# Key-value products in 32-column tiles, and one visit a period with outputs, key-value products and the next pair's scores

## The chip, the cores and the metric

The kernel runs on one core of a Trainium2 chip. The metric is the device time of one execution in microseconds, the median of three runs. Times from a profile are counted from the first instruction of the profiled execution.

## The reference

A linear attention with a decaying state (RWKV-5) is followed by a two-layer network with a leaky ReLU. Batch 4, 8 heads, 768 tokens, 48 channels a head; the network goes from 384 to 2048 and back to 384.

```python
state = np.zeros((B, H, D, D), dtype=np.float32)
for t in range(S):
    cur = np.einsum('bhd,bhe->bhde', u[None] * kt, vt)
    y[:, :, t] = np.einsum('bhd,bhde->bhe', rt, state + cur)
    state = w[None, :, :, None] * state + np.einsum('bhd,bhe->bhde', kt, vt)
...
h = x @ w_in
g = np.maximum(0.01 * h, h)
return (g @ w_out).astype(np.float32)
```

Here x holds y with the heads of a token side by side, and the output has 3072 rows of 384.

## The kernel before

The 768 tokens are cut into 6 chunks of 128, and a **stage** n (0 to 23) is one chunk of one batch element: chunk n // 4 of batch n % 4. So the state that stage n leaves is wanted by stage n + 4. A head's 48 channels are padded to 64 where two heads share the 128 rows of an operand, and four such pairs of heads make a stage.

The order of all work is written out by hand in the string ORDER (L27 to L52). Each word names a step and its stage; the steps are recorded in that order, each engine runs its own steps in that order, and `Sched` (L61) puts a semaphore wait before a step whose inputs, or whose buffer, belong to an earlier step of another engine. A wait holds up everything behind it on its engine. The steps that matter here:

- k, r, v (L241): loads, issued by GpSimd. P (L390): VectorE scales r and k by powers of the decay into `qk`. X (L395): SyncE issues a transposing DMA from `qk` to `tp`.
- A (L482): scores, 8 matmuls a stage on TensorE with 48 rows by 128 columns of weights, into two PSUM banks. M (L495): VectorE writes them masked into `at`, a half (a, b) at a time. Before that q (L419 to L423, VectorE) and Q (L430, GpSimd, two instructions of 128x512 a stage) have put the diagonal there.
- Y (L621): the outputs, 28 matmuls a stage with 128 rows by 32 columns of weights. They go round four groups of 32 columns of the array, so that four run side by side, each with 128 moving columns. y (L635): ScalarE copies them to `xT`.
- K (`kv_mm`, L516): the sums of key times value, 4 matmuls a stage (L523), one a pair of heads, with 128x128 weights and 96 moving columns. The off-diagonal blocks, of one head's key with the other's value, are computed too and are made zero later by the table `wl`. S (`state`, L580): VectorE adds the bank to the old state `st` (L589, 128x384) and multiplies by `wl` (L591) into the state of stage n + 4.
- J (L660): the first layer for a pair of stages, in eight parts of 6 matmuls with 256 moving columns; j (L671): ScalarE's leaky ReLU of each part into `gT`. H (L684): the second layer for one stage, 16 matmuls with 384 moving columns; h (L696): ScalarE's copy, and an output DMA issued by SyncE.

`take` (L213) hands out the PSUM bank that has been free longest, and `give` (L217) returns one when the step that reads it is recorded; so a J part can wait for the reader of the bank that it gets.

From stage 8 on two stages make a **period**: 2 A, 2 Y, 2 K, 2 H and 8 J on TensorE. In a period such as that of 10 and 11 the order on TensorE is H6, Y10 Y11, K10 K11, H7, J5.0 to J5.7, with the next scores A12 A13 after it; from the next period on, A14 A15 stand between J6.2 and J6.3. A run of steps Y, K or A between J and H is called a **visit** below. The order early in the kernel is not regular; around stages 6 and 7 it is Y7 y7 K5 r11 K6 S6 r10 k10 S5 Q9 v8 K7 S7 h0 h3 k11 J3.0.

Of the kernel before, what the change touches and what calls it, by code (L numbers as in the profile page):

```python
# [26 lines left out]
ORDER = """  # L27
w8 qk0 k0 v0z one r0 trow ones v0y tcol wlz r1 id8 F9 wi1 u8 zr table Cw Wl id E w bc lnw c0q@ T0q c0k@ tri u exps k1
T0k u16 wu8 Cu t0q t0k qtab P1q F6 k3 v3 U A0 ktab T1q v0 t1q X0 C D0 P1k T1k t1k F4 M0b P3k M0a T3k K3 utab X1 A1 D1
Q0 Y0 t3k P0k r3 P3q M1a T3q r2 P2q y0 k2 K0 M1b v1 Q1 W G0.1 Y1 t3q X3 wi3 A3 y1 g0.1 S3 T2q D3 G1.1 g1.1 k5 t2q r5 r4  # L30
P2k T2k wi2 S0 v2 M3b t2k Q3 G0.3 g0.3 G1.3 k4 M3a Y3 P5k A2 y3 P4q T4q v4 wi0 T5k v5 wo3 t4q g1.3 G3.1 q5 t5k Q5 G3.3
g3.3 P5q r6 wo2 X2 g3.1 M2b D2 wo1 G3.2 Q2 G0.2 g0.2 T5q t5q K2 P4k T4k M2a t4k S2 G1.2 g3.2 q4 Q4 K1 S1 Y2 A5 A4 G1.0
y2 G2.1 M5a G0.0 G2.3 M4a M5b Y5 g0.0 y5 M4b Y4 y4 G2.2 g2.2 K4 J2.4 j2.4 k6 wo0 J2.1 J2.2 g1.0 g1.2 S4 k7 P6q q6 j2.1
P6k P7k G2.0 r7 q7 X6T J2.6 j2.6 J2.3 j2.3 k8 G3.0 J2.7 j2.7 k9 r9 j2.2 J2.5 P7q g3.0 g2.3 X7T J2.0 H1 h1 r8 q8 g2.0 Q6
P9k j2.0 P8k H0 j2.5 H3 Q7 A6 P9q X9T P8q X8T v6 A7 M6a v7 M7a g2.1 H2 h2 v9 v11 v10 M6b Y6 M7b y6 Q8 q9 Y7 y7 K5 r11
K6 S6 r10 k10 S5 Q9 v8 K7 S7 h0 h3 k11 J3.0 j3.0 J3.1 j3.1 J3.2 j3.2 J3.3 j3.3 J3.4 j3.4 J3.5 j3.5 J3.6 j3.6 J3.7 j3.7
A8 A9 M8a M8b M9a M9b P10q P10k X10T P11q P11k X11T k12 r12 v12 k13 r13 v13 q10 Q10 q11 Q11 H4 h4 Y8 Y9 y8 y9 K8 K9 S8
S9 H5 h5 J4.0 j4.0 J4.1 j4.1 J4.2 j4.2 J4.3 j4.3 J4.4 j4.4 J4.5 j4.5 J4.6 j4.6 J4.7 j4.7 A10 A11 M10a M10b M11a M11b
P12q P12k X12T P13q P13k X13T k14 r14 v14 k15 r15 v15 q12 Q12 q13 Q13 H6 h6 Y10 Y11 y10 y11 K10 K11 S10 S11 H7 h7 J5.0
j5.0 J5.1 j5.1 J5.2 j5.2 J5.3 j5.3 J5.4 j5.4 J5.5 j5.5 J5.6 j5.6 J5.7 j5.7 A12 A13 M12a M12b M13a M13b P14q P14k X14T  # L40
P15q P15k X15T k16 r16 v16 k17 r17 v17 q14 Q14 q15 Q15 H8 h8 Y12 Y13 y12 y13 K12 K13 S12 S13 H9 h9 J6.0 j6.0 J6.1 j6.1
J6.2 j6.2 P16q P16k X16T P17q P17k X17T A14 A15 J6.3 j6.3 M14a M14b M15a M15b k18 r18 v18 k19 r19 v19 J6.4 j6.4 J6.5
j6.5 J6.6 j6.6 J6.7 j6.7 q16 Q16 q17 Q17 H10 h10 Y14 Y15 y14 y15 K14 K15 S14 S15 H11 h11 J7.0 j7.0 J7.1 j7.1 J7.2 j7.2
P18q P18k X18T P19q P19k X19T A16 A17 J7.3 j7.3 M16a M16b M17a M17b k20 r20 v20 k21 r21 v21 J7.4 j7.4 J7.5 j7.5 J7.6
j7.6 J7.7 j7.7 q18 Q18 q19 Q19 H12 h12 Y16 Y17 y16 y17 K16 K17 S16 S17 H13 h13 J8.0 j8.0 J8.1 j8.1 J8.2 j8.2 P20q P20k
X20T P21q P21k X21T A18 A19 J8.3 j8.3 M18a M18b M19a M19b k22 r22 v22 k23 r23 v23 J8.4 j8.4 J8.5 j8.5 J8.6 j8.6 J8.7
j8.7 q20 Q20 q21 Q21 H14 h14 Y18 Y19 y18 y19 K18 K19 S18 S19 H15 h15 J9.0 j9.0 J9.1 j9.1 J9.2 j9.2 P22q P22k X22T P23q
P23k X23T A20 A21 J9.3 j9.3 M20a M20b M21a M21b J9.4 j9.4 J9.5 j9.5 J9.6 j9.6 J9.7 j9.7 q22 Q22 q23 Q23 H16 h16 Y20 Y21
y20 y21 H17 h17 J10.0 j10.0 J10.1 j10.1 J10.2 j10.2 A22 A23 J10.3 j10.3 M22a M22b M23a M23b J10.4 j10.4 J10.5 j10.5
J10.6 j10.6 J10.7 j10.7 H18 h18 Y22 Y23 y22 y23 H19 h19 J11.0 j11.0 J11.1 j11.1 J11.2 j11.2 J11.3 j11.3 J11.4 j11.4  # L50
J11.5 j11.5 J11.6 j11.6 J11.7 j11.7 H20 h20 H21 h21 H22 h22
"""  # L52


# [89 lines left out]
def bass_rwkv5_eagle__then__act_leaky_relu_kernel(  # L144
# [370 lines left out]

    def kv_mm(n):  # L516
        iq = n % NQK
        ps_kv, key = kv_bank[n] = take()
        carried = NB <= n < CARRY

        def emit():
            for p in range(NP):
                last = PE.matmul(ps_kv[:, 96 * p:96 * p + 96],  # L523
                                 qk[iq][:, H + 2 * p:H + 2 * p + 2, :].rearrange("p h e -> p (h e)"),
                                 v_sb[:, n, :].rearrange("p (h e) -> p h e", e=E)[:, 2 * p:2 * p + 2, 0:D],
                                 start=p == 0 or not carried, stop=not carried)
# [52 lines left out]

    def state(n):  # L580
        ps_kv, key = kv_bank[n]
        give(key)
        kv = ps_kv[:, 0:HD].rearrange("p (m e) -> p m e", e=2 * D)
        new = st[(n + NB) % NT]
        if n < NB or n < CARRY:
            add("dve", lambda: V.tensor_tensor(new[:, :, :], kv, wl[:, :, :], ALU.mult),
                R=[key, "wl0", "wl1"], W=[("st", (n + NB) % NT)])
        else:
            add("dve", lambda: V.tensor_tensor(sum_t[n % 4][:, :, :], kv, st[n % NT][:, :, :], ALU.add),  # L589
                R=[key, ("st", n % NT)], W=[("sum", n % 4)])  # L590
            add("dve", lambda: V.tensor_tensor(new[:, :, :], sum_t[n % 4][:, :, :], wl[:, :, :], ALU.mult),  # L591
                R=[("sum", n % 4), "wl0", "wl1"], W=[("st", (n + NB) % NT)])
# [212 lines left out]
```

## Time and profile before

| | |
|---|---|
| median of three runs | 168.86 us (168.78 to 168.94) |
| span of the profiled execution | 166.8 us, first to last instruction |
| PE busy | 160.2 us, 96% of the span |
| VectorE (DVE), GpSimd (POOL), ScalarE (ACT) busy | 107.6, 111.0, 89.0 us |
| granted TensorE clock | 1.000 over the span |

The runs' times are taken without a profile; what the profiled execution took in all is not listed beside its span of 166.8 us; the median of the runs lies 2.0 us above that span. PE in the profile is TensorE's matmuls and PEld its weight loads. Matmuls are pipelined: a row's duration holds the time that a matmul takes through the array (some 0.2 us) beside its share of the stream, so distances between starts tell the rate. A row "x8" in a timeline reaches from the first start to the last end of eight.

### The profile page before, as it was taken

The numbers are of one execution on the slowest core, as the hardware profiler recorded it, in microseconds if no ns is written. First come the engines' busy times: TensorE is split into PE (matmuls) and PEld (weight loads), VectorE is DVE, ScalarE is ACT, GpSimd is POOL, SyncE is SP. The second block draws the span as 40 slices with busy tenths as digits, with TensorE's granted clock in tenths as the row PEclk, the third lists the DMA queues.
The fourth block names the chain that finished last, engine by engine and source line by source line (L and its number), as shares of the span: only waits on it lengthen the run. The fifth ranks groups of instructions, "written<-read, shape, count | busy, mean of one in ns | idle before, by whom it ended". The sixth has DMA issues, their size and how long they took to land.

```text
span 166.8 us, 4840 instructions
## 1 busy us (share of the span) xinstructions
PE 160.2 (96%) x2076; PEld 120.6 (72%) x2076; DVE 107.6 (64%) x224; ACT 89.0 (53%) x168; POOL 111.0 (67%) x125
## 2 busy tenths in 40 slices
PE   2899989999999999999999999999999999999994
PEld 2578879986567678678678678678678678678663
DVE  7799998478687695695699998865765705000000
ACT  3846973875048339339337437437437447449121
POOL 8999898978999949859759979896630630000000
PEclk9999999999999999999999999999999999999999
DMA  7999999999999994996994999999917011011012
GB/s 109 156 140 157 169 193 192 171 149 173 93 168 220 113 157 130 105 108 155 105 146 118 152 127 127 156 140 140 154 51 165 12 47 51 0 47 51 35 59 96
DMA packets 101267, 20.18 MB, mean 121 GB/s; under 512 B 94459, under 2 KB 101246, under 8 KB 101246
## 3 DMA queue, kind: packets, MB, share of 16 engines
q0 software_dynamic: 76512, 10.03, 95.0%
q1 hardware_dynamic: 23694, 9.65, 29.1%
q8 instruction: 16, 0.26, 0.7%
q10 hardware_dynamic: 1040, 0.20, 0.6%
q14 instruction: 5, 0.04, 0.1%
HBM read 20.45 MB, written 4.72 MB: 151 GB/s over the span
## 4 chain that ended last, share of the span: by engine, by line
PE 86%; POOL 7%; DMA 3%; DVE 2%; issue 0%; ACT 0%; POOLq 0%
PE ps L684 38%; PE ps L660 36%; PE ps L621 6%; DMA r_sb<-in_r_dram 3%; PE ps L482 3%; PE ps L523 2%; POOL r_sb L241 2%; POOL k_sb L241 2%; POOL v_sb L241 2%; POOL w_in_sb L251 1%; DVE prod L405 1%; DVE s_tok L423 0%; PE ps L453 0%; POOL trow L273 0%; DVE rku L421 0%
## 5 line engine op out<-in xcount | busy, mean ns | idle before, releaser
L660 PE MATMUL ps<-xT,w_in_sb 128*128 128x256 bf16 (+1 forms) x672 | 67.2, 257 | 0.0
L684 PE MATMUL ps<-w_out_sb,gT 128*128 128x384 bf16 (+2 forms) x400 | 65.6, 320 | 0.0
L671 ACT ACTIVATE gT<-ps 128x512 bf16<-128x512 f32 x96 | 56.3, 598 | 13.8 <-PE ps L660 9.7
L660 PEld LDWEIGHTS ps<-xT,w_in_sb 128*128 128x128 bf16 x672 | 57.1, 98 | 7.5 <-DVE sum_t L589 0.5
L430 POOL TENSOR_TENSOR at<-ident,s_tok 128x512 bf16<-128x512 bf16 x40 | 42.7, 1096 | 23.4 <-DVE s_tok L423 23.4
L684 PEld LDWEIGHTS ps<-w_out_sb,gT 128*128 128x128 bf16 x400 | 37.7, 98 | 22.4
L696 ACT ACTIVATE out_sb<-ps 128x384 f32<-128x384 f32 (+2 forms) x25 | 11.8, 477 | 54.5 <-PE ps L684 54.5
L495 DVE CAST_PREDICATED at<-mask,ps 128x512 bf16<-128x512 uint16 x40 | 24.9, 684 | 21.3 <-PE ps L482 21.2
L241 POOL DMA_DIRECT2D v_sb<-in_v_dram x24 | 22.1, 927 | 0.0
L241 POOL DMA_DIRECT2D k_sb<-in_k_dram x23 | 21.2, 925 | 0.0
L241 POOL DMA_DIRECT2D r_sb<-in_r_dram x23 | 21.1, 924 | 0.1
L421 DVE TENSOR_TENSOR rku<-r_sb,ku 128x384 bf16<-128x384 bf16 x20 | 13.8, 688 | 1.1 <-DMA r_sb<-in_r_dram 0.5
L589 DVE TENSOR_TENSOR sum_t<-ps,st 128x384 bf16<-128x384 f32 x16 | 8.8, 550 | 5.6 <-PE ps L523 5.6
L635 ACT ACTIVATE xT<-ps 128x384 bf16<-128x384 f32 x24 | 10.8, 490 | 2.6 <-PE ps L621 2.6
L423 DVE TENSOR_REDUCE s_tok<-rku 128x8 f32<-128x384 bf16 x20 | 11.1, 553 | 0.7
L591 DVE TENSOR_TENSOR st<-sum_t,wl 128x384 bf16<-128x384 bf16 x16 | 10.6, 664 | 0.6
L621 PE MATMUL ps<-at,v_sb 128*32 128x128 bf16 x384 | 10.8, 223 | 0.0
L390 DVE TENSOR_TENSOR qk<-k_sb,ktab 128x384 bf16<-128x384 bf16 x23 | 10.1, 444 | 1.1 <-DMA k_sb<-in_k_dram 1.1
L621 PEld LDWEIGHTS ps<-tp,st 128*32 128x32 bf16 x240 | 7.3, 96 | 3.0 <-issue 1.6
L621 PEld LDWEIGHTS ps<-at,v_sb 128*32 128x32 bf16 x384 | 8.8, 98 | 0.5 <-issue 0.2
L621 PE MATMUL ps<-tp,st 128*32 128x128 bf16 x240 | 9.1, 221 | 0.0
L390 DVE TENSOR_TENSOR qk<-r_sb,qtab 128x384 bf16<-128x384 bf16 x23 | 8.8, 386 | 0.2 <-DMA r_sb<-in_r_dram 0.2
(63 smaller groups left out, 92.9 us busy)
## 6 DMA issues: line engine op xcount, KB each, us to landing
out_dram<-out_sb SPq DMA_DIRECT2D x23, 192.0 KB, 2.2
v_sb<-in_v_dram POOLq DMA_DIRECT2D x24, 96.0 KB, 4.8
r_sb<-in_r_dram POOLq DMA_DIRECT2D x23, 96.0 KB, 4.7
k_sb<-in_k_dram POOLq DMA_DIRECT2D x23, 96.0 KB, 4.9
w_in_sb<-in_moe_w_in_dram POOLq DMA_DIRECT2D x4, 384.0 KB, 6.1
w_out_sb<-in_moe_w_out_dram POOLq DMA_DIRECT2D x4, 384.0 KB, 7.1
tp<-qk SPq DMA_TRANSPOSE x18, 5.3
k_f<-in_k_dram ACTq DMA_DIRECT2D x1, 192.0 KB, 2.8
```

Source lines behind the costliest of these rows:

```text
L241: add("pool", lambda: G.dma_start(dst, src), R=pace, W=[(which, n)], dma=f"{which}{n}")
L390: add("dve", lambda: V.tensor_tensor(qk[iq][:, H * half:H * half + H, 0:D], hd(src), hd(tab[:, :]), ALU.mult), R=[(name, n), "qk"[half] + ...
L421: add("dve", lambda: V.tensor_tensor(rku[i2][:, :], r_of(n), ku[i2][:, :], ALU.mult), R=[("r", n), ("ku", i2)], W=[("rku", i2)])
L423: add("dve", lambda: V.tensor_reduce(s_tok[i2][:, :], hd(rku[i2][:, :]), AX.X, ALU.add), R=[("rku", i2)], W=[("s", i2)])
L430: add("pool", lambda hh=hh, s_of=s_of: G.tensor_tensor(at[ia][:, hh, :, :], ident[:, :].unsqueeze(1).to_broadcast([128, NP, 128]), s_of.un ...
L495: add("dve", lambda: V.copy_predicated(at[n % NAT][:, hh, :, :], mask[:, :].bitcast(mybir.dt.uint16).unsqueeze(1).to_broadcast([128, NP, 1 ...
L621: last = PE.matmul(ps_y[32 * q:32 * q + 32, 128 * s:128 * s + 128], a, m, start=not whole and step == 0, stop=step == len(columns[q]) - 1)
L635: add("act", lambda: A.activation(xT[ix][:, :, 128 * slot:128 * slot + 128], ps_y[:, 0:HD].rearrange("p (s t) -> p s t", t=128), AF.Copy), ...
L660: last = PE.matmul(ps_g[:, step * f:step * f + step], w_in_sb[:, s, 128 * fb:128 * fb + 128], xT[ix][:, s, t], start=s == 0, stop=s == NSL ...
L671: add("act", lambda: A.activation(gT[ig][:, fb0:fb0 + count, t], ps_g[:, :].rearrange("p (f t) -> p f t", t=128 * width), AF.Prelu, alpha= ...
L684: last = PE.matmul(ps_o[:, 0:c1 - c0], gT[ig][:, s, 128 * slot:128 * slot + 128], w_out_sb[:, s, c0:c1], start=s == 0, stop=s == NFB - 1)
L696: add("act", lambda: A.activation(out_sb[io][:, c0:c1], ps_o[:, 0:c1 - c0], AF.Copy), R=[key], W=held)
```

## The change

Three things are changed. From stage 6 on (`STRIPS = 6`) K is made of 16 matmuls a stage instead of 4: weights of 128 rows by 32 columns, 48 moving columns, one head each, going round the four 32-column groups. Two stages share a bank, the even one in columns 0 to 191 and the odd one in columns 192 to 383; the bank is given back by the odd stage's S. S works on the diagonal blocks alone, in two halves of 64 partitions: two additions and two multiplications of 64x192 in place of one and one of 128x384. The ring of state buffers has 6 instead of 10, since only the first six get zeros outside the blocks.

```diff
-    NQK, NTP, NVS, NAT, NT, NX, NG, NO = 6, 6, 6, 6, 10, 2, 2, 4
+    NQK, NTP, NVS, NAT, NT, NX, NG, NO = 6, 6, 6, 6, 6, 2, 2, 4
...
     def kv_mm(n):
         iq = n % NQK
-        ps_kv, key = kv_bank[n] = take()
+        kv_bank[n] = kv_bank[n - 1] if n >= STRIPS and n % 2 else take()
+        ps_kv, key = kv_bank[n]
...
+        def strips():
+            c0 = NP * D * (n % 2)
+            for p in range(NP):
+                for q in range(4):
+                    h = 2 * p + q // 2
+                    last = PE.matmul(ps_kv[32 * q:32 * q + 32, c0 + D * p:c0 + D * p + D],
+                                     qk[iq][:, H + h, 32 * (q % 2):32 * (q % 2) + 32], v_sb[:, n, E * h:E * h + D],
+                                     start=True, stop=True)
+            return last
...
     def state(n):
         ps_kv, key = kv_bank[n]
+        new = st[(n + NB) % NT]
+        if n >= STRIPS:
+            if n % 2:
+                give(key)
+            c0 = NP * D * (n % 2)
+            kv, both = ps_kv[:, c0:c0 + NP * D].rearrange("p (m e) -> p m e", e=D), sum_t[n % 4]
+            for hh in range(2):
+                part = (slice(64 * hh, 64 * hh + 64), slice(None), slice(D * hh, D * hh + D))
+                add("dve", lambda part=part: V.tensor_tensor(both[part], kv[part[0]], st[n % NT][part], ALU.add),
+                    R=[key, ("st", n % NT)], W=[("sum", n % 4, hh)])
+            for hh in range(2):
+                part = (slice(64 * hh, 64 * hh + 64), slice(None), slice(D * hh, D * hh + D))
+                add("dve", lambda part=part: V.tensor_tensor(new[part], both[part], wl[part], ALU.mult),
+                    R=[("sum", n % 4, hh), f"wl{hh}"], W=[("st", (n + NB) % NT)])
+            return
```

The order is the same up to J4.7, and again from J10.4 on. Between them both H of a period come first, then one visit with Y, K and the next pair's A, then J. The period of stages 12 and 13, before and after (it begins and ends within lines of ORDER):

```diff
-H8 h8 Y12 Y13 y12 y13 K12 K13 S12 S13 H9 h9 J6.0 j6.0 J6.1 j6.1
-J6.2 j6.2 P16q P16k X16T P17q P17k X17T A14 A15 J6.3 j6.3 M14a M14b M15a M15b k18 r18 v18 k19 r19 v19 J6.4 j6.4 J6.5
-j6.5 J6.6 j6.6 J6.7 j6.7 q16 Q16 q17 Q17
+H8 h8 H9 h9 Y12 Y13 y12 y13 K12 K13 A14 A15 M14a
+M14b M15a M15b P16q P16k X16T P17q P17k X17T q16 q17 J6.0 j6.0 J6.1 j6.1 k18 r18 v18 k19 r19 v19 Q16 Q17 S12 S13 J6.2
+j6.2 J6.3 j6.3 J6.4 j6.4 J6.5 j6.5 J6.6 j6.6 J6.7 j6.7
```

A10 A11 keep a visit of their own, now behind P12 P13 q12 q13 on VectorE. Six visits are merged: Y10 to K11 with A12 A13, and so on to Y18 to K19 with A20 A21, and Y20 Y21 with A22 A23 (no K is left there). Y8 Y9 K8 K9 stay where they were, and so do K5, K6 and K7.

More of the change, by code (lines that the diff above doesn't have):

```diff
@@ L26 @@
 TURNED, DIAG, CARRY, EXACT, RAW = 6, 4, 4, 1, 1
+STRIPS = 6
 ORDER = """
@@ L29 @@
 T0k u16 wu8 Cu t0q t0k qtab P1q F6 k3 v3 U A0 ktab T1q v0 t1q X0 C D0 P1k T1k t1k F4 M0b P3k M0a T3k K3 utab X1 A1 D1
[L30 to L38, printed above, removed]
@@ L39 @@
-P12q P12k X12T P13q P13k X13T k14 r14 v14 k15 r15 v15 q12 Q12 q13 Q13 H6 h6 Y10 Y11 y10 y11 K10 K11 S10 S11 H7 h7 J5.0
-j5.0 J5.1 j5.1 J5.2 j5.2 J5.3 j5.3 J5.4 j5.4 J5.5 j5.5 J5.6 j5.6 J5.7 j5.7 A12 A13 M12a M12b M13a M13b P14q P14k X14T
-P15q P15k X15T k16 r16 v16 k17 r17 v17 q14 Q14 q15 Q15 H8 h8 Y12 Y13 y12 y13 K12 K13 S12 S13 H9 h9 J6.0 j6.0 J6.1 j6.1
-J6.2 j6.2 P16q P16k X16T P17q P17k X17T A14 A15 J6.3 j6.3 M14a M14b M15a M15b k18 r18 v18 k19 r19 v19 J6.4 j6.4 J6.5
-j6.5 J6.6 j6.6 J6.7 j6.7 q16 Q16 q17 Q17 H10 h10 Y14 Y15 y14 y15 K14 K15 S14 S15 H11 h11 J7.0 j7.0 J7.1 j7.1 J7.2 j7.2
@@ L44 @@
[L44 to L48, printed above, removed]
@@ L49 @@
-y20 y21 H17 h17 J10.0 j10.0 J10.1 j10.1 J10.2 j10.2 A22 A23 J10.3 j10.3 M22a M22b M23a M23b J10.4 j10.4 J10.5 j10.5
-J10.6 j10.6 J10.7 j10.7 H18 h18 Y22 Y23 y22 y23 H19 h19 J11.0 j11.0 J11.1 j11.1 J11.2 j11.2 J11.3 j11.3 J11.4 j11.4
-J11.5 j11.5 J11.6 j11.6 J11.7 j11.7 H20 h20 H21 h21 H22 h22
+Q0 Y0 t3k P0k r3 P3q M1a T3q r2 P2q y0 k2 K0 M1b v1 Q1 W G0.1 Y1 t3q X3 wi3 A3 y1 g0.1 S3 T2q D3 G1.1 g1.1 k5 t2q r5
+r4 P2k T2k wi2 S0 v2 M3b t2k Q3 G0.3 g0.3 G1.3 k4 M3a Y3 P5k A2 y3 P4q T4q v4 wi0 T5k v5 wo3 t4q g1.3 G3.1 q5 t5k Q5
@@ new lines @@
+G3.3 g3.3 P5q r6 wo2 X2 g3.1 M2b D2 wo1 G3.2 Q2 G0.2 g0.2 T5q t5q K2 P4k T4k M2a t4k S2 G1.2 g3.2 q4 Q4 K1 S1 Y2 A5 A4
+G1.0 y2 G2.1 M5a G0.0 G2.3 M4a M5b Y5 g0.0 y5 M4b Y4 y4 G2.2 g2.2 K4 J2.4 j2.4 k6 wo0 J2.1 J2.2 g1.0 g1.2 S4 k7 P6q q6
+j2.1 P6k P7k G2.0 r7 q7 X6T J2.6 j2.6 J2.3 j2.3 k8 G3.0 J2.7 j2.7 k9 r9 j2.2 J2.5 P7q g3.0 g2.3 X7T J2.0 H1 h1 r8 q8
+g2.0 Q6 P9k j2.0 P8k H0 j2.5 H3 Q7 A6 P9q X9T P8q X8T v6 A7 M6a v7 M7a g2.1 H2 h2 v9 v11 v10 M6b Y6 M7b y6 Q8 q9 Y7 y7
+K5 r11 K6 S6 r10 k10 S5 Q9 v8 K7 S7 h0 h3 k11 J3.0 j3.0 J3.1 j3.1 J3.2 j3.2 J3.3 j3.3 J3.4 j3.4 J3.5 j3.5 J3.6 j3.6
@@ new lines @@
+J3.7 j3.7 A8 A9 M8a M8b M9a M9b P10q P10k X10T P11q P11k X11T k12 r12 v12 k13 r13 v13 q10 Q10 q11 Q11 H4 h4 Y8 Y9 y8
+y9 K8 K9 S8 S9 H5 h5 J4.0 j4.0 J4.1 j4.1 J4.2 j4.2 J4.3 j4.3 J4.4 j4.4 J4.5 j4.5 J4.6 j4.6 J4.7 j4.7 P12q P12k X12T
+P13q P13k X13T q12 q13 A10 A11 M10a M10b M11a M11b k14 r14 v14 k15 r15 v15 Q12 Q13 H6 h6 H7 h7 Y10 Y11 y10 y11 K10 K11
+A12 A13 M12a M12b M13a M13b P14q P14k X14T P15q P15k X15T q14 q15 J5.0 j5.0 J5.1 j5.1 k16 r16 v16 k17 r17 v17 Q14 Q15
+S10 S11 J5.2 j5.2 J5.3 j5.3 J5.4 j5.4 J5.5 j5.5 J5.6 j5.6 J5.7 j5.7 H8 h8 H9 h9 Y12 Y13 y12 y13 K12 K13 A14 A15 M14a
@@ new lines @@
+M14b M15a M15b P16q P16k X16T P17q P17k X17T q16 q17 J6.0 j6.0 J6.1 j6.1 k18 r18 v18 k19 r19 v19 Q16 Q17 S12 S13 J6.2
+j6.2 J6.3 j6.3 J6.4 j6.4 J6.5 j6.5 J6.6 j6.6 J6.7 j6.7 H10 h10 H11 h11 Y14 Y15 y14 y15 K14 K15 A16 A17 M16a M16b M17a
+M17b P18q P18k X18T P19q P19k X19T q18 q19 J7.0 j7.0 J7.1 j7.1 k20 r20 v20 k21 r21 v21 Q18 Q19 S14 S15 J7.2 j7.2 J7.3
+j7.3 J7.4 j7.4 J7.5 j7.5 J7.6 j7.6 J7.7 j7.7 H12 h12 H13 h13 Y16 Y17 y16 y17 K16 K17 A18 A19 M18a M18b M19a M19b P20q
+P20k X20T P21q P21k X21T q20 q21 J8.0 j8.0 J8.1 j8.1 k22 r22 v22 k23 r23 v23 Q20 Q21 S16 S17 J8.2 j8.2 J8.3 j8.3 J8.4
@@ new lines @@
+j8.4 J8.5 j8.5 J8.6 j8.6 J8.7 j8.7 H14 h14 H15 h15 Y18 Y19 y18 y19 K18 K19 A20 A21 M20a M20b M21a M21b P22q P22k X22T
+P23q P23k X23T q22 q23 J9.0 j9.0 J9.1 j9.1 Q22 Q23 S18 S19 J9.2 j9.2 J9.3 j9.3 J9.4 j9.4 J9.5 j9.5 J9.6 j9.6 J9.7 j9.7
+H16 h16 H17 h17 Y20 Y21 y20 y21 A22 A23 M22a M22b M23a M23b J10.0 j10.0 J10.1 j10.1 J10.2 j10.2 J10.3 j10.3 J10.4
+j10.4 J10.5 j10.5 J10.6 j10.6 J10.7 j10.7 H18 h18 Y22 Y23 y22 y23 H19 h19 J11.0 j11.0 J11.1 j11.1 J11.2 j11.2 J11.3
+j11.3 J11.4 j11.4 J11.5 j11.5 J11.6 j11.6 J11.7 j11.7 H20 h20 H21 h21 H22 h22
@@ L517, in kv_mm @@
         iq = n % NQK
-        ps_kv, key = kv_bank[n] = take()
+        kv_bank[n] = kv_bank[n - 1] if n >= STRIPS and n % 2 else take()
+        ps_kv, key = kv_bank[n]
         carried = NB <= n < CARRY
+        def strips():
[7 more added lines that the diff above has]
+            return last
         def emit():
+            if n >= STRIPS:
+                return strips()
             for p in range(NP):
@@ L581, in state @@
         ps_kv, key = kv_bank[n]
+        new = st[(n + NB) % NT]
+        if n >= STRIPS:
+            if n % 2:
[11 more added lines that the diff above has]
+            return
         give(key)
         kv = ps_kv[:, 0:HD].rearrange("p (m e) -> p m e", e=2 * D)
-        new = st[(n + NB) % NT]
         if n < NB or n < CARRY:
@@ L589, in state @@
             add("dve", lambda: V.tensor_tensor(sum_t[n % 4][:, :, :], kv, st[n % NT][:, :, :], ALU.add),
-                R=[key, ("st", n % NT)], W=[("sum", n % 4)])
+                R=[key, ("st", n % NT)], W=[("sum", n % 4, 0), ("sum", n % 4, 1)])
             add("dve", lambda: V.tensor_tensor(new[:, :, :], sum_t[n % 4][:, :, :], wl[:, :, :], ALU.mult),
-                R=[("sum", n % 4), "wl0", "wl1"], W=[("st", (n + NB) % NT)])
+                R=[("sum", n % 4, 0), "wl0", "wl1"], W=[("st", (n + NB) % NT)])
     def y_mm(n, ps_y, key):
```

## The prediction

> **What bounds the kernel now.** I read the busy times and the chain of waits on the profile's page first, then windows of one period each (the numbers after the time are busy us of PE, PEld, DVE, ACT, POOL).
>
> ```profile
> PE 160.2 (96%) x2076; PEld 120.6 (72%) x2076; DVE 107.6 (64%) x224; ACT 89.0 (53%) x168; POOL 111.0 (67%) x125
> PE 86%; POOL 7%; DMA 3%; DVE 2%; issue 0%; ACT 0%; POOLq 0%
> ...
> 87.28:99.72 12.44, 12.44 (x162) 9.25 (x161) 12.17 (x23) 6.61 (x12) 11.55 (x13) 1.00 1.62 132
> 99.72:112.16 12.44, 12.44 (x162) 9.23 (x161) 9.90 (x23) 6.61 (x12) 11.90 (x14) 1.00 1.61 143
> 112.16:124.60 12.44, 12.44 (x162) 9.24 (x161) 8.37 (x19) 6.61 (x12) 7.45 (x8) 1.00 1.32 120
> ```
>
> TensorE sets the end: 12.44 us of 12.44 in a period. VectorE comes near once (12.17). The chain in order of time (start, length, what) gives one period's parts, and two undisturbed lengths from the tail:
>
> ```profile
> 99.72 1.97 PE ps L660 x18
> 101.68 0.55 PE ps L482 x16
> 102.24 3.38 PE ps L660 x30
> 105.62 2.60 PE ps L684 x16
> 108.22 0.90 PE ps L621 x56
> 109.11 0.45 PE ps L523 x8
> 109.56 2.60 PE ps L684 x16
> ...
> 148.80 5.24 PE ps L660 x48
> ```
>
> Starts within TensorE's timeline, and the durations of single matmuls (ns, min/median/max), give each kind's own rate:
>
> ```profile
> L482 PE MATMUL ps<-tp x192: 216/216/311, 8.5 to 139.0; 48*128 48x128 bf16 x192
> L523 PE MATMUL ps<-v_sb,qk x80: 206/206/287, 10.8 to 121.8; 128*128 128x96 bf16 x80
> L621 PE MATMUL ps<-at,v_sb x384: 219/219/314, 12.3 to 145.9; 128*32 128x128 bf16 x192
> L510 PE MATMUL ps<-wu,prod x16: 163/165/211, 9.4 to 21.7; 128*128 128x2 bf16 x16
> ...
> 21.60 0.25 PE L510 MATMUL ps<-wu,prod 128*128 128x2 bf16 x4 [0.58 <-DVE prod L405]
> ...
> 96.05 0.23 PE L621 MATMUL ps<-at,v_sb 128*32 128x128 bf16 x4
> 96.11 0.23 PE L621 MATMUL ps<-tp,st 128*32 128x128 bf16 x4
> 96.16 0.23 PE L621 MATMUL ps<-at,v_sb 128*32 128x128 bf16 x4
> ...
> 96.44 0.23 PE L621 MATMUL ps<-at,v_sb 128*32 128x128 bf16 x4
> 96.60 0.51 PE L523 MATMUL ps<-v_sb,qk 128*128 128x96 bf16 x8
> ...
> 101.62 0.62 PE L482 MATMUL ps<-tp 48*128 48x128 bf16 x16
> ```
>
> A: (0.62 - 0.216) / 15 = 27 ns. K: (0.51 - 0.206) / 7 = 43 ns, 0.35 us a pair of stages. Y: a group of four every 55 ns, the four starting within 0.01 us (0.23 - 0.219); 14 groups, 0.77 us. J: 5.24 / 48 = 109 ns. H: 2.60 us where it follows K. At these rates a period would take 5.24 + 5.20 + 0.43 + 0.77 + 0.35 = 11.99 us; the chain's seven pieces sum to 12.45. The other 0.46 us lies where the shape of the weights changes: J to A, A to J, H to Y, Y to K. K to H, 128x128 both, costs nothing. So a change of shape costs about **0.11 us**.
>
> **Part 1, one visit instead of two.** After the change a merged period has H to Y, K to A and A to J; Y to K is no change any more, since both use 128x32. Three changes instead of four: -0.11 us for each of six merged visits (the sixth, without K, had J to A, A to J, H to Y, Y to H and gets three too): **-0.66**. If the drain comes at every new accumulation rather than at a new shape, it is 0. The visit of 8 and 9 gains Y to K and loses K to H5: nothing.
>
> What is queued now behind this visit is J. It needs both y, which H used to cover. ScalarE's rows, before:
>
> ```profile
> 95.87 0.49 ACT L696 ACTIVATE out_sb<-ps 128x384 f32<-128x384 f32 x1 [2.06 <-PE ps L684]
> 96.33 0.88 ACT L635 ACTIVATE xT<-ps 128x384 bf16<-128x384 f32 x2
> ```
>
> The second y ends at 97.21. Seen on that clock, K would start at 96.50, take 0.22 (next part), A would start at 96.83, and J at 96.83 + 0.43 + 0.11 = 97.37: hidden, with some 0.1 us to spare. Only in the sixth visit A starts at 96.60 and J could go at 97.14, while y ends at 97.21 and its signal takes about 0.05: **+0.12**. The A that is moved needs the transposes X, whose landing takes (us):
>
> ```profile
> DMA to landing us min/median/max: 3.1/5.3/7.9
> ```
>
> They are now issued behind M of the pair before, ahead of the next two output DMAs in SyncE's queue, with a J and two H (10.4 us) until A. GpSimd's loads stand ahead of Q as before and are wanted a period later. M's four masks come behind A; the first J part whose bank a mask frees is J.3, 3 x 0.655 = 1.97 us after J.0. All of that is hidden while VectorE keeps up (below).
>
> **Part 2, the strips.** 32 matmuls a pair in 8 groups of four. No row has 128x32 weights with 48 columns. From below: the cost per column between K (96, 43 ns) and J (256, 109 ns) is 0.41 ns, which gives 24 ns for 48. From above: Y's group, 55 ns, in case loading the weights sets its pace. The nearest row for a matmul too short for its stream to count is L510: (0.25 - 0.165) / 3 = 28 ns from start to start. I take 28: 8 x 0.028 = 0.22 us against 0.35, -0.12 a pair, for six pairs (8/9 to 18/19) **-0.74** (from -0.94 at 24 to +0.54 at 55).
>
> The Trainium skill speaks against this part: "TensorEngine Tiling (Array Packing)", section Instruction Overhead, says that a matmul has about 60 cycles of overhead, so that 1 column takes as long as 60, and that no tiling factor should be taken from a dimension already small. With 60 cycles per group of four at the 2.4 GHz of the Trainium skill ("TensorE: Matmul & The Clock Gate", its first table), an estimate from these two pages of it, a group would take 25 ns, and six pairs would give -0.9: the rule bites only if the four tiles don't overlap.
>
> **Part 3, the shared bank at stages 6 and 7.** K7 writes the bank that S6 reads, and is recorded behind S6: TensorE waits there for both halves of S6's addition, with K7, H and all of J3 behind it. Rows around it:
>
> ```profile
> 48.82 0.68 PE L523 MATMUL ps<-v_sb,qk 128*128 128x96 bf16 x12
> 49.37 2.08 POOL L430 TENSOR_TENSOR at<-ident,s_tok 128x512 bf16<-128x512 bf16 x2
> 49.37 0.56 DVE L589 TENSOR_TENSOR sum_t<-ps,st 128x384 bf16<-128x384 f32 x1 [0.47 <-PE ps L523]
> 49.48 5.71 PE L660 MATMUL ps<-xT,w_in_sb 128*128 128x256 bf16 x48
> 49.96 1.71 DVE L591 TENSOR_TENSOR st<-sum_t,wl 128x384 bf16<-128x384 bf16 x1
> ...
> 52.45 0.55 DVE L589 TENSOR_TENSOR sum_t<-ps,st 128x384 bf16<-128x384 f32 x1
> 53.03 0.36 DVE L591 TENSOR_TENSOR st<-sum_t,wl 128x384 bf16<-128x384 bf16 x1
> 53.05 1.86 PEld L660 LDWEIGHTS ps<-xT,w_in_sb 128*128 128x128 bf16 x18 [0.31 <-DVE sum_t L589]
> ...
> L568 DVE CAST wu<-ps 48x4 bf16<-48x4 f32 x2 | 0.3, 158 | 0.0
> ```
>
> K5 ends its starts at 48.95, K6 goes from 49.09 (a change of shape) to 49.18 and is out 0.2 later, so S6 adds from 49.42. One addition of 192 columns: 158 ns for 4 columns and 550 for 384 give 0.35 us, two give 0.71 (0.56 if halving halves them, 1.10 if it doesn't). K7 starts at about 50.17, J3.0 at 50.17 + 0.11 + 0.11 = 50.39, 0.9 us after its 49.48. Part comes back: J3 lost (5.71 - 0.27) - 47 x 0.109 = 0.3 us to waits for S5's and S7's banks. Now the multiplication held by GpSimd ends near 51.7 still, S5 and S7 have added by about 53.5, and J3.5 wants that bank at 50.39 + 5 x 0.655 = 53.7. Net **+0.6** (+0.4 to +1.3).
>
> S's halves make 4 x 0.35 - 2 x 0.55 + 4 x 0.26 - 2 x 0.36 = 0.6 us more VectorE work a period (0.26 for half a 0.36 multiplication, by the same 0.16 fixed); taken as hidden, since S is wanted a period later. The smaller ring only reuses states read a period before.
>
> **Sum:** -0.66 + 0.12 - 0.74 + 0.6 = -0.7 us on the span of 166.8, which becomes 166.1. The 2.0 us between span and median are taken as fixed: **168.2 us**.
>
> **Rivals.** *Strips at Y's pace* (55 ns): -0.66 + 0.12 + 0.54 + 0.6 = +0.6, 169.5. It decides at 43 ns a group, where the strips gain nothing. For it: weights of the same shape; against: Y's 55 ns is what 128 columns at 0.41 take anyway.
>
> *VectorE becomes the bound,* and J.3 waits for the first mask:
>
> ```profile
> L495 DVE CAST_PREDICATED at<-mask,ps 128x512 bf16<-128x512 uint16 x40 | 24.9, 684 | 21.3 <-PE ps L482 21.2
> ...
> 94.95 2.33 DVE L421 TENSOR_TENSOR rku<-r_sb,ku 128x384 bf16<-128x384 bf16 x1
> ...
> 104.91 0.36 DVE L421 TENSOR_TENSOR rku<-r_sb,ku 128x384 bf16<-128x384 bf16 x1
> ```
>
> 12.17 + 0.6 = 12.8 us of work in a period of 12.2 make it 0.6 later each time. The first mask (0.68, begun half an A ahead of J.0) ends some 0.35 after J.0, which leaves 1.97 - 0.35 = 1.6 us; that is used up after three of the five periods, and the last two cost 0.6 each: 168.2 + 1.2 = 169.4. It decides where VectorE's work passes 12.2 us a period. Against: 9.90 and 8.37 in the next two windows; the 12.17 hold a multiplication of q of 2.33 us that takes 0.36 elsewhere.
>
> *The drain stays between Y and K.* -0.7 + 6 x 0.11 = 0.0: 168.8, the change giving nothing. By the Trainium skill, "TensorEngine Tiling (Array Packing)", section Key Properties, this falls: only a change of the tiling mode drains the array, not one of the tile. No row here has two kinds of work of one shape next to each other but K and H.
>
> *Cheaper than taken:* strips at 24 ns, +0.4 at stage 6: -1.1, 167.8.
>
> *One start at a time:* 32 starts of 28 ns are 0.90 us a pair, +0.55 each for six and the wait unchanged: 168.86 + 3.4 = 172.2. Against: four Y starts within 0.01 us. The Trainium skill, "TensorE: Matmul & The Clock Gate", section Wait — 56ns, not 53.3ns?, puts such a floor (about 25 ns) under every start; for Y's tiles the trace disagrees.
>
> **How the numbers follow.** Forecast (167.9 to 168.5): 0.52. Cheaper: 0.15. Drain stays, or strips near 43 ns (168.5 to 169.1): 0.13. Strips at Y's pace: 0.10. VectorE: 0.07. One start at a time: 0.03. About 0.2%, 0.34 us, can be told from no change: faster 0.68, same 0.13, slower 0.19. The range 167.5 to 169.1 leaves out the last three.
>
> **What would show it.** L523's strips: their group spacing, and no gap ahead of them behind L621; one A piece a period, 0.55 long, with an undivided 5.24 J behind it; TensorE waiting for DVE sum_t just ahead of K7, near 50. If PE is idle in a merged period, or waits for L495 or L635 by more than 0.1, the prediction is wrong there.

## The result

The changed kernel takes 182.05 us in the median (181.62 to 183.82 over six runs), against 168.9 us for the kernel before: a ratio of 1.076 (95% interval 1.071 to 1.082). It was predicted at 168.2 us, somewhat faster. The profiled execution took 181.91 us. Three of the ten runs of e2 and one of the twelve of e6, below, fell in a slower state, and the figures given for e2 and e6 are those of the other runs.

The page of the changed kernel, beside its busy times and its chain of waits (lines have moved: J is L688, H is L712, Y is L649, A is L483; the strips are L528, whole K is L537, the half additions and multiplications of S are L604 and L608, whole ones L617 and L619, the masks L496, q's L422 and L424):

```profile
span 180.1 us, 5209 instructions
PE 162.5 (90%) x2244; PEld 122.0 (68%) x2244; DVE 113.9 (63%) x252; ACT 89.3 (50%) x168; POOL 110.7 (61%) x125
PE 64%; DVE 27%; DMA 3%; issue 3%; POOL 1%; ACT 0%; DVEq 0%; POOLq 0%
```

TensorE was 86% of the chain that ended last and is 64% now; VectorE has gone from 2% to 27%. TensorE is busy only 2.3 us longer than before, in a span 13.3 us longer: the rest is waiting, or matmuls that ran slower. Whom TensorE waits for (engine, tile, line; in total, times, longest):

```profile
PE ps L712 <- DVE sum_t L604: 9.0, 5, 2.0
...
PE ps L483 <- DMA tp<-qk: 1.0, 1, 1.0
PE ps L528 <- DVE sum_t L604: 0.9, 1, 0.9
```

H waits five times for an addition of S, the first time for 1.0 us and then for 2.0. That wait was not in the prediction at all; TensorE idle in a merged period was, as a sign that it would be wrong. VectorE's timeline in one period, and TensorE's second H behind it:

```profile
91.25 2.48 DVE L496 CAST_PREDICATED at<-mask,ps 128x512 bf16<-128x512 uint16 x4 [3.87 <-PE ps L483]
...
96.36 1.08 DVE L422 TENSOR_TENSOR rku<-r_sb,ku 128x384 bf16<-128x384 bf16 x1
97.47 0.55 DVE L424 TENSOR_REDUCE s_tok<-rku 128x8 f32<-128x384 bf16 x1
97.94 0.73 DVE L604 TENSOR_TENSOR sum_t<-ps,st 64x192 bf16<-64x192 f32 x2
98.71 1.77 DVE L608 TENSOR_TENSOR st<-sum_t,wl 64x192 bf16<-64x192 bf16 x2
100.51 0.74 DVE L604 TENSOR_TENSOR sum_t<-ps,st 64x192 bf16<-64x192 f32 x2
101.28 0.52 DVE L608 TENSOR_TENSOR st<-sum_t,wl 64x192 bf16<-64x192 bf16 x2
...
96.55 2.76 PE L712 MATMUL ps<-w_out_sb,gT 128*128 128x384 bf16 x16
101.31 2.77 PE L712 MATMUL ps<-w_out_sb,gT 128*128 128x384 bf16 x16 [2.00 <-DVE sum_t L604]
```

From the first mask at 91.25 VectorE works without a pause through masks, P, q and both S, and the odd stage's addition ends at 101.25, exactly 10 us later. The second H could have gone at 99.3 and starts at 101.31. The link is not data: H reads nothing of S. `take` hands the second H the bank that the odd S gives back, since that has become the oldest on the list there (H9 gets the bank of K10 and K11). In the order before no H of a period came to S's banks; late J parts or the next A did (J5.5 and J5.6, A15, A17, A19, A21).

So a loop closes: addition, H, Y, K, A, masks, P, q, S and the next addition, and the period is as long as the loop. Windows of two such periods (busy us of PE, PEld, DVE, ACT, POOL, granted clock, DMA share, GB/s):

```profile
89.66:104.08 14.42, 12.43 (x191) 9.22 (x193) 10.23 (x22) 6.61 (x12) 9.49 (x11) 1.00 1.05 106
...
132.90:148.96 16.06, 14.07 (x191) 9.70 (x193) 10.23 (x22) 6.61 (x12) 4.22 (x4) 0.89 0.26 58
```

14.42 us instead of 12.44, with neither engine full. The second window is longer still: in TensorE's timeline its late H took 4.42 us instead of 2.77,

```profile
144.54 4.42 PE L712 MATMUL ps<-w_out_sb,gT 128*128 128x384 bf16 x16 [1.99 <-DVE sum_t L604]
```

and a window over its second part shows a granted clock of 0.52 (the number behind POOL's):

```profile
146.00:149.00 3.00, 3.00 (x18) 1.20 (x20) 0.00 (x0) 0.00 (x0) 0.00 (x0) 0.52 0.00 0
```

The sum, from one start of Y to another: the five periods from Y10 (75.01) to Y20 (148.89) take 73.9 us, where the kernel before takes 5 x 12.44 = 62.2. That is 11.7 us more: 1.65 by the slow H, and some 2.0 in each period. A13's wait adds little, since it lies in the first of these periods (75.01 to 89.59), whose H waits 1.0 us instead of 2.0:

```profile
86.89 2.77 PE L712 MATMUL ps<-w_out_sb,gT 128*128 128x384 bf16 x16 [1.02 <-DVE sum_t L604]
```

K7's wait comes to 0.7 us net: Y6 to Y8 takes 11.14 us instead of 10.47. The last 1.0 us had been lost before that, since Y6 starts at 48.91 instead of 47.92. Up to there the order of work is that of before, and in the eleven profiles of this case Y6 starts anywhere from 47.9 to 49.1; so this part is put down to the execution, not to the change. 11.7 + 0.7 + 1.0 = 13.4, against 13.3 us.

### The profile page after: what moved, and what is told of

The parts are those of the page before. It is cut to its first block, busy times and chain, and to the rows that moved or that the text cites. A ratio compares the mean times of both kernels' runs of the same rounds, so it can differ in the third digit from the quotient of the medians.

```text
span 180.1 us, 5209 instructions
## 1 busy us (share of the span) xinstructions
PE 162.5 (90%) x2244; PEld 122.0 (68%) x2244; DVE 113.9 (63%) x252; ACT 89.3 (50%) x168; POOL 110.7 (61%) x125
## 4 chain that ended last, share of the span: by engine, by line
PE 64%; DVE 27%; DMA 3%; issue 3%; POOL 1%; ACT 0%; DVEq 0%; POOLq 0%
PE ps L712 29%; PE ps L688 21%; DVE at L496 6%; PE ps L649 6%; DVE st L608 5%; DVE sum_t L604 4%; DVE rku L422 4%; DMA k_sb<-in_k_dram 3%; DVE qk L391 3%; PE ps L483 3%; DVE s_tok L424 3%; PE ps L454 2%; DVE ku L420 2%; PE ps L528 1%; PE ps L537 1%
## 5 line engine op out<-in xcount | busy, mean ns | idle before, releaser
L712 PE MATMUL ps<-w_out_sb,gT 128*128 128x384 bf16 (+2 forms) x400 | 67.1, 325 | 9.0 <-DVE sum_t L604 9.0
L688 PE MATMUL ps<-xT,w_in_sb 128*128 128x256 bf16 (+1 forms) x672 | 67.0, 259 | 0.7 <-issue 0.7
L688 PEld LDWEIGHTS ps<-xT,w_in_sb 128*128 128x128 bf16 x672 | 57.8, 99 | 7.3 <-issue 0.8
L431 POOL TENSOR_TENSOR at<-ident,s_tok 128x512 bf16<-128x512 bf16 x40 | 42.2, 1084 | 32.3 <-DVE s_tok L424 32.3
L712 PEld LDWEIGHTS ps<-w_out_sb,gT 128*128 128x128 bf16 x400 | 38.2, 99 | 34.2 <-DVE sum_t L604 10.9
L496 DVE CAST_PREDICATED at<-mask,ps 128x512 bf16<-128x512 uint16 x40 | 25.0, 685 | 26.6 <-PE ps L483 26.4
L608 DVE TENSOR_TENSOR st<-sum_t,wl 64x192 bf16<-64x192 bf16 x28 | 15.3, 545 | 0.6
L422 DVE TENSOR_TENSOR rku<-r_sb,ku 128x384 bf16<-128x384 bf16 x20 | 12.2, 611 | 2.5 <-DMA r_sb<-in_r_dram 1.8
L424 DVE TENSOR_REDUCE s_tok<-rku 128x8 f32<-128x384 bf16 x20 | 11.1, 553 | 0.7
L649 PE MATMUL ps<-at,v_sb 128*32 128x128 bf16 x384 | 10.8, 223 | 0.0
L604 DVE TENSOR_TENSOR sum_t<-ps,st 64x192 bf16<-64x192 f32 x28 | 9.9, 353 | 1.2 <-PE ps L528 0.6
L649 PEld LDWEIGHTS ps<-tp,st 128*32 128x32 bf16 x240 | 7.3, 96 | 3.3 <-issue 2.8
L483 PE MATMUL ps<-tp 48*128 48x128 bf16 x192 | 8.4, 225 | 1.0 <-DMA tp<-qk 1.0
L649 PEld LDWEIGHTS ps<-at,v_sb 128*32 128x32 bf16 x384 | 8.8, 98 | 0.6 <-issue 0.4
L649 PE MATMUL ps<-tp,st 128*32 128x128 bf16 x240 | 9.1, 221 | 0.0
```

The lines of the kernel that those rows point to most:

```text
L422: add("dve", lambda: V.tensor_tensor(rku[i2][:, :], r_of(n), ku[i2][:, :], ALU.mult), R=[("r", n), ("ku", i2)], W=[("rku", i2)])
L424: add("dve", lambda: V.tensor_reduce(s_tok[i2][:, :], hd(rku[i2][:, :]), AX.X, ALU.add), R=[("rku", i2)], W=[("s", i2)])
L431: add("pool", lambda hh=hh, s_of=s_of: G.tensor_tensor(at[ia][:, hh, :, :], ident[:, :].unsqueeze(1).to_broadcast([128, NP, 128]), s_of.un ...
L496: add("dve", lambda: V.copy_predicated(at[n % NAT][:, hh, :, :], mask[:, :].bitcast(mybir.dt.uint16).unsqueeze(1).to_broadcast([128, NP, 1 ...
L604: add("dve", lambda part=part: V.tensor_tensor(both[part], kv[part[0]], st[n % NT][part], ALU.add), R=[key, ("st", n % NT)], W=[("sum", n ...
L608: add("dve", lambda part=part: V.tensor_tensor(new[part], both[part], wl[part], ALU.mult), R=[("sum", n % 4, hh), f"wl{hh}"], W=[("st", (n ...
```

## The experiments

In e1 to e4 one part is taken away or put back; e5 to e7 go on from there; e8 puts the suspected wait back alone; e9 is the second remedy. Line numbers in their profiles are those of the changed kernel.

**e1, K's own bank.** The shared bank of the strips stays with K.

```diff
-        kv_bank[n] = kv_bank[n - 1] if n >= STRIPS and n % 2 else take()
+        kv_bank[n] = kv_bank[n - 1] if n >= STRIPS and n % 2 else own.pop() if own else take()
...
             if n % 2:
-                give(key)
+                own.append(kv_bank[n])
```

> The changed kernel, with one difference: the bank that the pairs of K share never goes back to the common list; K takes it again two stages later. VectorE's work and the order of all steps stay. Theory (the second H of a period waits for the bank that S's addition reads, and that addition is at the end of VectorE's queue): no H waits for the addition any more, a merged period is about 12.2 us instead of 14.4, the clock stays at 1.000, and the time is about 168.4 us (167.9 to 168.9). Rival (VectorE's chain of masks, scaling, row sums and state updates is itself too long for the period, whoever has the bank): the time stays above 179 us.

Measured: 170.3 us (170.07 to 171.47), ratio 1.008 (1.005 to 1.012). No H waits for S, and the clock is 1.000. A window of one period:

```profile
102.02:114.26 12.24, 12.24 (x185) 9.28 (x186) 10.22 (x23) 6.61 (x12) 9.49 (x11) 1.00 1.37 125
```

TensorE's waits that are left behind the start of the kernel:

```profile
PE ps L483 <- DMA tp<-qk: 1.3, 1, 1.3
PE ps L528 <- DVE sum_t L604: 0.9, 1, 0.9
```

The period is 12.24 us with VectorE's 10.22 us of work unchanged. So VectorE's work fits, and the rival falls: what cost 2 us a period was the bank. The time lies 1.4 us above the range; the two waits above are what is left, and A13's 1.3 us, which the expectation did not have, are about that much.

**e2, S ahead of P and q.** Common list of banks, another place for S. The lines are pieces of ORDER, from one of the five periods.

```diff
-M14a M14b M15a M15b P16q P16k X16T P17q P17k X17T q16 q17 J6.0 j6.0 J6.1 j6.1
...
-Q16 Q17 S12 S13 J6.2
+M14a M14b M15a M15b S12 S13 P16q P16k X16T P17q P17k X17T q16 q17 J6.0 j6.0 J6.1 j6.1
...
+Q16 Q17 J6.2
```

> The changed kernel with the common list of banks as it is; in the five merged periods with K the two S stand directly behind the masks, ahead of P and q. Theory (the wait is for a late addition): the bank is free some 4 us after A instead of 10, ahead of any step that gets it, and the time is about 168.4 us (167.9 to 169.2). Rival (VectorE's total of 10.2 us a period): still above 179 us, since the total is the same.

Measured: 170.91 us (170.07 to 172.2), ratio 1.011 (1.007 to 1.015). The profiled execution, the fastest, has periods of 12.25 us:

```profile
89.77:102.02 12.25, 12.25 (x187) 9.31 (x186) 9.08 (x23) 6.61 (x12) 8.49 (x10) 1.00 1.38 128
```

No H waits for S. VectorE's work is 9.08 us instead of 10.22: the even stage's two multiplications take 0.52 us, ahead of GpSimd's Q, and took 1.77 in the changed kernel, where Q ran beside them. The total is again above the expected range, and the same two waits are there in the profiled execution (A13's 1.5 us, K7's 0.9); why other runs took up to 2.1 us more than that one is open.

**e3, the order alone.**

```diff
-STRIPS = 6
+STRIPS = 99
```

K has 128x128 weights and a bank a stage, S works on the whole state.

> The new order alone: no strips at any stage, K with 128x128 weights and a bank of its own for each stage, S on the whole state. Theory: the loss comes with the order, not with the strips or with the sharing. By the list of banks the first H of a period then gets the bank of the even stage's S and the second that of the odd one's; the even addition ends some 7.4 us after A, then two H, Y, K and A take 7.0: a period of 14.4 to 14.6 us and 181 to 183 us in all. Rival (the strips, by the shared bank, make the wait): below 170 us.

Measured: 178.96 us (178.67 to 179.81), ratio 1.058 (1.052 to 1.064). The first H of a period is late now, and both run on from there:

```profile
127.03 5.38 PE L712 MATMUL ps<-w_out_sb,gT 128*128 128x384 bf16 x32 [1.84 <-DVE sum_t L617]
141.48 0.82 PE L712 MATMUL ps<-w_out_sb,gT 128*128 128x384 bf16 x4 [1.84 <-DVE sum_t L617]
```

141.48 - 127.03 = 14.45 us a period, as expected; the expected total was too high, since five times 2.0 on 168.9 is 178.9. The loss comes with the order. Strips and sharing only decide which H waits.

**e4, the strips alone.** The order is that of the kernel before, all else is as changed.

> The strips, the shared bank and the six state buffers alone, with the order of before. Theory: a pair of K takes 0.25 us instead of 0.35 (0.6 us saved over six pairs), the change of shape only moves from in front of K to behind it, and K7 waits for S6's addition with TensorE idle for 0.9 us, of which some comes back: 168.9 us (168.5 to 169.4). Rival (strips are the dear part): above 172 us.

Measured: 171.06 us (170.42 to 171.73), ratio 1.011 (1.008 to 1.014): 2 us above the expectation. The profiled execution is the slowest, 171.73 us. Its waits:

```profile
PE ps L483 <- DVE sum_t L604: 1.1, 1, 1.1
PE ps L528 <- DVE sum_t L604: 0.9, 1, 0.9
...
PE ps L688 <- DVE sum_t L617: 0.3, 1, 0.3
```

K7's wait is as expected; a second one had been missed: a second A, which in that order gets the bank of an odd S, waits 1.1 us once. It is the same mechanism at another place. The chain of waits shows the rest ahead of J3.5, which starts at 55.33 (53.06 in the kernel before):

```profile
50.99 2.38 DVE st L608
...
55.33 2.14 PE ps L688 x18
```

S6's first half multiplication took 2.38 us there, with GpSimd's Q beside it from 51.17 to 53.25, where a free one takes 0.26; and the additions of S5 and S7, whose banks J3 wants, stand behind it: J3 had not been rid of its waits in this run. So what K7's wait was thought to give back can be lost again: Y6 to Y8 takes 12.18 us here, 1.7 more than in the kernel before. The strips themselves do gain: two periods without a wait, Y8 to Y10 and Y10 to Y12, take 12.35 us each instead of 12.44.

**e5, own bank, strips from stage 8 on.**

```diff
-STRIPS = 6
+STRIPS = 8
```

> The changed kernel with K's own bank, and strips from stage 8 on (K6 and K7 with 128x128 weights and a bank each). Theory: the wait of 0.9 us ahead of K7 is gone, of which J3's waits for the banks of S5 and S7 take some 0.3 back, so about 0.6 us below the kernel with the own bank alone: 169.6 us (169.2 to 170.1). A13 still waits some 1.3 us for its transpose. Rival (the wait of K7 was covered by J3's waits): 170.3 us as with the own bank alone.

Measured: **168.28 us** (167.87 to 169.56), ratio 0.996 (0.993 to 0.999): faster than the kernel before, and 2.0 us below e1 where 0.6 was expected. K7's wait is gone. A13's is 0.2 us instead of 1.3, though nothing was done about it:

```profile
PE ps L483 <- DMA tp<-qk: 0.2, 1, 0.2
```

The two account for the difference between the profiled executions (spans of 168.2 and 166.4 us): Y6 to Y8 takes 10.19 us instead of 11.15, and Y10 to Y12 12.62 instead of 13.76, while Y6 started 0.28 us later. In the chain of waits the transpose of that visit took 7.90 us in e1 and 6.76 here:

```profile
68.42 6.76 DMA tp<-qk
75.17 0.14 issue
```

Why it was faster is open. A13 waits 1.0, 1.3 and 1.5 us in the changed kernel, e1 and e2, with strips from stage 6 on, and 0.2, 0.6 and 0.4 us in e5, e8 and e9, with strips from stage 8 on.

**e6, earlier transposes.** P12, X12, P13 and X13 are moved ahead of S8 and S9 (in e5's order they stand behind J4.7). The lines are pieces of ORDER.

```diff
-K8 K9 S8 S9 H5 h5
...
-J4.7 j4.7 P12q P12k X12T P13q P13k X13T q12 q13 A10 A11
+K8 K9 P12q P12k X12T P13q P13k X13T S8 S9 H5 h5
...
+J4.7 j4.7 q12 q13 A10 A11
```

> The same with P12, X12, P13 and X13 ahead of S8 and S9 on VectorE, some 4 us earlier. Theory (the rest of the loss is the first merged visit, where A13 waits for a transposing DMA that was issued 5 to 8 us before): no wait at A13, TensorE busy without a gap from J3 to the end, 1.3 us less than the run before it: 168.3 us (167.9 to 168.8). Rival (the transpose is slow whenever it is issued there, as loads and outputs run beside it): 169.6 us.

Measured: 169.88 us (169.51 to 170.4), ratio 1.006 (1.004 to 1.008): worse than e5 by 1.6 us. A13 doesn't wait, but Y does:

```profile
PE ps L649 <- ACT out_sb L724: 1.1, 1, 1.1
...
PE ps L649 <- DVE at L496: 0.6, 1, 0.6
```

VectorE's timeline ahead of it:

```profile
69.63 2.89 DVE L422 TENSOR_TENSOR rku<-r_sb,ku 128x384 bf16<-128x384 bf16 x1
73.14 2.48 DVE L496 CAST_PREDICATED at<-mask,ps 128x512 bf16<-128x512 uint16 x4
```

Moved work met GpSimd's Q: one multiplication of q took 2.89 us, with Q beside it from 70.19 to 72.29, instead of 1.08 at that place in e5; the masks of stage 10 began at 73.1 instead of 70.9, and Y10 and Y11 waited for them (the releaser ACT in the first row had long been done; it is the masks that came last). Both the theory and its rival missed this.

**e7, the merged visit with whole K.** As e6, with K and S as in the kernel before and two banks kept for K.

```diff
-STRIPS = 8
+STRIPS = 99
...
-        kv_bank[n] = kv_bank[n - 1] if n >= STRIPS and n % 2 else own.pop() if own else take()
+        kv_bank[n] = kv_bank[n - 1] if n >= STRIPS and n % 2 else own.pop(0) if own and n >= 8 else take()
...
-        give(key)
+        own.append(kv_bank[n]) if n >= 8 else give(key)
```

> As the run before it, but K with 128x128 weights at all stages, each stage's bank kept for K, S on the whole state. Theory: a pair of K takes 0.35 us instead of 0.25 (six pairs, 0.6 us) and five merged visits have a fourth change of shape, Y to K, of 0.11 us: 1.1 us above the run before it, 169.4 us (169.0 to 170.0), near the kernel before. Rival (strips gain nothing on TensorE): no difference from the run before it.

Measured: 168.73 us (168.3 to 170.29), ratio 1.000 (0.997 to 1.002): below the expected range and below e6, whose waits of Y are not there. The comparison with e6 is spoilt by e6's own waits; that with e5, whose merged periods have no wait either, is by the period:

```profile
100.32:112.76 12.44, 12.44 (x162) 9.35 (x162) 9.22 (x19) 6.61 (x12) 9.60 (x11) 1.00 1.32 124
```

12.44 us, just as before the change, against 12.24 in e5. So one visit alone gives nothing with 128x128 weights in K (four changes of shape either way), and strips are worth 0.20 us a period in the merged order: 0.10 by their rate and 0.10 by the change of shape that they save.

**e8, the wait alone.** e5, with H9, H11, H13, H15 and H17 made to wait for the odd stage's addition, whose bank and data they do not use.

```diff
-        add("pe", emit, R=[("gT", ig, slot, fb) for fb in range(NFB)] + [("wout", i) for i in range(4)], W=[key])
+        add("pe", emit, R=[("gT", ig, slot, fb) for fb in range(NFB)] + [("wout", i) for i in range(4)]
+            + ([("sum", (n + 2) % 4, 1)] if n in (9, 11, 13, 15, 17) else []), W=[key])
```

> The kernel with the own bank and strips from stage 8 on (168.28 us), and one wait more: in the five merged periods with K the second H is made to wait for the odd stage's addition, though its bank is free. All steps, banks and data stay. Theory (this one wait is the loss of the change): H starts some 2 us late in each of five periods, a period is 14.4 us instead of 12.25, and the time is 168.3 + 5 x 2.15 = 179.0 us (178.3 to 182, the upper part if the clock falls after a wait as it did in the changed kernel). Rival (the loss came from the sharing of banks at large, so that taking K's bank out of the list removed more than this wait): below 174 us.

Measured: 182.58 us (182.44 to 183.1), ratio 1.080 (1.076 to 1.084). One added wait makes the fastest kernel here as slow as the changed one.

Its waits, and three of the late H in its chain of waits:

```profile
PE ps L712 <- DVE sum_t L604: 9.6, 5, 2.1
```

```profile
100.55 4.44 PE ps L712 x16
...
116.72 2.76 PE ps L712 x16
...
131.22 4.44 PE ps L712 x16
```

From 116.72 to 131.22 it is 14.5 us, 2.26 more than e5's 12.24, and twice H took 4.44 us instead of 2.76, at a lower clock. The first period, Y10 to Y12, takes 14.49 us, 1.9 more than in e5. 4 x 2.26 + 1.9 + 2 x 1.68 = 14.3, which is the difference to e5. The time is 0.6 above the top of the expected range; the clock fell twice here.

**e9, S behind the masks, strips from stage 8 on, common banks.** e2 with `STRIPS = 8`.

> The common list of banks, strips from stage 8 on, and S directly behind the masks in the merged periods. Theory (either remedy ends the wait, an own bank or an early addition): periods of 12.25 us and 168.3 us (167.8 to 169.0). Rival (a bank in the common list still costs something elsewhere, at the J part that gets it): above 169.5 us.

Measured: 168.41 us (167.98 to 169.34), ratio 0.997 (0.995 to 0.999). A13 waits 0.4 us; from there on the chain of waits runs through TensorE, with periods of 12.25 us:

```profile
88.20 5.35 PE ps L688 x48
93.55 5.20 PE ps L712 x32
...
100.45 5.35 PE ps L688 x48
```

Either remedy will do. Both beat the kernel before by 0.3 to 0.4%.

## Why the prediction was wrong

The step that failed is the cost of S's late place on VectorE in the new order, a term that the prediction put at nothing. Part 1 calls the transposes, the loads and the masks hidden "while VectorE keeps up" and does not speak of S; of S itself it says near the end of part 3: "taken as hidden, since S is wanted a period later". That holds for the state which S writes. It was never asked who wants the bank that S reads. For the masks the prediction did ask ("the first J part whose bank a mask frees is J.3"), and for K7 it did; for S it stopped at the data. What the runs showed in its place is a wait of 2.0 us a period, of the second H for the bank that the odd S reads. The extra 0.6 us of VectorE's work, which that sentence is about, is not needed for it: e3 has a loss of 2.0 us a period without them, by the order alone. The list of banks could have been followed by hand, and then the lengths compared. From A on VectorE does the masks, P, q and S in a row, and the odd addition ends 10.0 us behind the first mask in the changed kernel; J starts 0.05 us behind the first mask (91.25, 91.30), so the second H stands 0.05 + 5.35 + 2.6 = 8.0 us behind it. Whatever hands it a bank that is read until 10.0 makes it 2 us late. e8 shows the price of that one link, and e1, e2, e5 and e9 that it goes when the link or the late addition goes.

The rival "VectorE becomes the bound" was near it and wrong in its terms. It asked whether VectorE's work passes 12.2 us a period; the work is 10.23 us and fits, as e1 shows with the same 10.22. A loop through both engines can set the period though each has time to spare: 10.0 us of VectorE behind A, then H, Y, K and the first A, 2.77 + 0.90 + 0.25 + 0.35, and signals of some 0.1: 14.4.

The other steps, one by one:

- *One visit, -0.66 by one change of shape less each.* Right with strips: the merged periods of e1 and e5 take 12.24 us, where the forecast's terms give 12.45 - 0.11 - 0.12 = 12.22. It is the strips that save the change: the visit alone gives 0.00 (e7) and the strips alone 0.09 us a period (e4), and together they give 0.20.
- *Strips, 28 ns a group, 0.22 us a pair.* The mechanism was right, and the size a little off. In the changed kernel's timeline, K between the last Y and A:

```profile
90.33 0.23 PE L649 MATMUL ps<-at,v_sb 128*32 128x128 bf16 x4
90.39 0.42 PE L528 MATMUL ps<-v_sb,qk 128*32 128x48 bf16 x32
90.74 0.62 PE L483 MATMUL ps<-tp 48*128 48x128 bf16 x16
```

  and the durations of one strip:

```profile
L528 PE MATMUL ps<-v_sb,qk x224: 182/183/197, 50.1 to 133.9; 128*32 128x48 bf16 x112
```

  (0.42 - 0.183) / 31 = 7.6 ns a matmul, 31 ns a group, 0.25 us a pair. K starts 0.06 behind the last group of Y, that is without a change of shape, and A starts 0.35 behind K, 0.10 more than K's own 0.25, with one. "Strips at Y's pace", "the drain stays" and "one start at a time" have all fallen. The Trainium skill, "TensorE: Matmul & The Clock Gate", section Wait — 56ns, not 53.3ns?, has no two starts closer than about 25 ns; between tiles of 32 columns the trace disagrees, with 7.6 ns.
- *K7 behind S6, +0.6.* Right in the changed kernel, e1 and e2, where it is 0.7 (Y6 to Y8), though 1.7 in e4. TensorE's rows, with VectorE's additions between:

```profile
50.08 0.28 PE L528 MATMUL ps<-v_sb,qk 128*32 128x48 bf16 x16
50.44 0.74 DVE L604 TENSOR_TENSOR sum_t<-ps,st 64x192 bf16<-64x192 f32 x2 [0.55 <-PE ps L528]
51.24 0.28 PE L528 MATMUL ps<-v_sb,qk 128*32 128x48 bf16 x16 [0.88 <-DVE sum_t L604]
51.45 5.41 PE L688 MATMUL ps<-xT,w_in_sb 128*128 128x256 bf16 x48
```

  Two half additions take 0.74 us (0.71 forecast), and J3 runs 5.41 us without the waits that had made it 5.71.
- *The sixth visit waits for y, +0.12.* Right. The chain of waits of e1, where J takes 5.35 us behind the other visits:

```profile
138.50 0.04 issue
138.55 5.42 PE ps L688 x48
```

  0.04 and 0.07, 0.11 us.
- *Transposes hidden.* Wrong for the first merged visit, where P12 and P13 come behind S8, S9 and GpSimd's Q: A13 waited 1.0 us in the changed kernel, 1.3 in e1 and 1.5 in e2. The forecast had only looked at a regular period.

With the waits on the bank and at K7 gone and little left of A13's, the change gives 168.28 against 168.95 in the same comparison (e5), -0.7 us. That this is the forecast's -0.7 is chance: the forecast had K7's wait still in.

## What to carry to other kernels

When work is moved, ask for every step on the way two things: who wants what it writes, and who gets the buffer that it reads. With a list that hands out the oldest free buffer, a reordering changes the second answer at every step behind it, so write the list out for the new order and look for takers that stand ahead of a late reader. And two engines with time to spare can still form a loop that is longer than the work of either; the sum of the loop, not the share of busy time, is then the period.

## What was not expected of the hardware

The granted clock fell to 0.52 for some 3 us behind some of these waits and not behind others. In the profiled executions it fell behind one of the four waits of 2.0 us in the changed kernel, behind two of the four of 2.1 us in e8, and behind none of the five of 1.84 us in e3. Each fall cost 1.65 us or so, as H took 4.42 or 4.44 us instead of 2.77. It explains part of the spread of the changed kernel too: the mean granted clock was 0.991 in four of its six runs, the profiled one among them, and 0.98 in the two longest (183.19 and 183.82 us), as two falls would give. What decides whether a wait is followed by a fall is open. The Trainium skill, "TensorE: Matmul & The Clock Gate", section Part 1: The HAM clock gate (the "warmup" mystery), gives half rate after an idle window of about 3.4 us, a window that runs freely; the traces here show falls after 2.0 us idle, and that not every wait of that length is followed by one.
